# The second product of a sine block, from sixteen full pieces to seven half-size products

## The chip, the cores and the metric

The kernel runs on one core of a Trainium2 chip. The metric is the device time of one execution in microseconds (us), the median of several runs. TensorE (PE) multiplies, VectorE (DVE), ScalarE (ACT) and GpSimd (POOL) work on elements, SyncE (SP) issues nearly all DMA transfers; SBUF is the working memory on the chip, PSUM takes the sums of PE in eight banks of 128 x 512 floats.

## The reference

Block-local attention over 64-token chunks gives `x` (4608 tokens x 512). Then `u = ((x @ w1) * (x @ w2)) @ w3 @ w_o`, and the part that is changed here, the sine block:

```python
def _moe2_ref(x, w_in, w_out):
    h = x @ w_in                      # 4608 x 512 @ 512 x 2048
    g = h * np.cos(h)
    return (g @ w_out).astype(np.float32)   # 4608 x 2048 @ 2048 x 512
```

All weights come as 64-bit floats and are decoded on the chip. For precision every operand of a product is split into two float16 halves, high and low, and a product is three matmuls: high x high, low x high, high x low.

## The kernel before

The 4608 tokens are nine blocks of 512. Three kinds of work follow each other and overlap at their borders: attention with the first products (`ab`, `u_of`) for all blocks, then the sine blocks. Between them `w_in` and `w_out` are surveyed (largest value) and converted to float16 halves in DRAM (`convert_in`, `convert_out`).

A sine block has two products. The first, `h_of`, is by seven half-size products (the scheme of Winograd and Strassen): `u` is combined into seven operands by `combined`, the seven operands of `w_in` are made once and fetched again for every block (`fetch_in`, 896 KB a transfer). Per block there are four steps `f_`; a step makes seven products of 12 matmuls with 256 columns into the banks x, y, z of `ps_h`. ACT copies a partial result from PSUM to SBUF (`kept`, L1278), DVE adds another one from PSUM (`plus`, L1284), and so arise four quarters c11, c21, c22, c12 of `h`. `finish` then makes g = h cos(h) of each quarter: round with a magic number (ACT L1296), subtract (DVE L1300), absolute value (L1306, or ACT L1304), sine (ACT L1309), multiply (L1312, on DVE or POOL), and two halves in float16 (ACT L1315, DVE L1318).

The second product, `y_of`, is plain: 4 tiles of 128 tokens x 16 pieces of `w_out` x 3 matmuls with 512 columns (L1351 to L1353), 192 a block, into two banks; ACT scales the sum (L1358), SP stores it (L1361). All of `w_out` lies in SBUF (32 KB of each partition, `wout_p`), fetched once by `fetch`; `gh_p` holds g of two blocks.

Nothing is ordered by hand: every operation is recorded by `op(engine, cost, priority, ...)`, and `Plan.order` places all of them by a list schedule with the costs given in the code (`MM`, `LAT`, `ISSUE`, `DMA_RATE`), the priorities and the free places of the buffer pools. The order of each engine that comes out is fixed; on the chip an engine runs its queue in that order and waits on semaphores. y of a block is placed among the first product of the next block by its priority (`start_h`, `period`, `Y0`).

Of the kernel before, what the change touches and what calls it, by code (L numbers as in the profile page):

```python
# [11 lines left out]
F32 = mybir.dt.float32  # L12
# [11 lines left out]
MAGIC = 12582912.0  # L24

# [39 lines left out]
class Plan:  # L65
# [50 lines left out]
    def order(self):  # L116
# [26 lines left out]
        now, done, wakes, order, on_psum = 0.0, 0, [0.0], [], False  # L143
# [12 lines left out]
        while done < len(ops):  # L156
# [11 lines left out]
            for e in ENGINES:  # L168
# [35 lines left out]
                if e == "DVE":  # L204
                    if not o.psum:
                        o.cost += SHARED * max(0.0, free["POOL"] - now)
                    on_psum = o.psum
                elif e == "POOL" and free["DVE"] > now and not on_psum:
                    o.cost += SHARED * (free["DVE"] - now)
# [7 lines left out]
                for s in o.succ:  # L217
                    s.left -= 1
                    there = end if list(s.alts) == [e] and e != "SP" else end + LAT[e]
                    s.ready = max(s.ready, there)  # L220
                    if not s.left:
                        for a in s.alts:
                            heapq.heappush(pending[a], (s.ready, s.prio, s.n))
                        heapq.heappush(wakes, s.ready)
                for b in o.bufs:
                    left[id(b)] -= 1
                    ends[id(b)] = max(ends.get(id(b), 0.0), end + LAT[e])
# [28 lines left out]
def fused_kernel(  # L256
# [36 lines left out]
    R0, R1, C0, C1, A0, A1, A2, A3, I0, I1, I2, I3, I4, I5, F0, F1, Y0 = 0.9, 10.9, 16.5, 27.6, 60.0, 6, 70.0, 10.6, 240.5, 10.0, 28.1, 510.5, 5.6, 11.6, 8.4, -26.5, 55.8  # L293
# [69 lines left out]
    ps_h = bank_pool(0, 1, 2, 3, 4, 5, queue=True)  # L363
    ps_y = bank_pool(6, 7)
# [26 lines left out]
    def operand(a):  # L391
# [4 lines left out]
        operand, *line("XHL", 0, 2 * KB, 7), *line("W12", 52 * KB, 2 * KB, 2), *line("RES", 10 * KB, 2 * KB, 3), *line("WG", 32 * KB, 2 * KB, 4), queue=True  # L396
# [16 lines left out]
    wout_p = sbuf_pool(halves_of, ("CONV", 0, 32 * KB))  # L413
    uin_p = sbuf_pool(chunks, ("XHL", 14 * KB, 8 * KB), queue=True)
    gh_p = sbuf_pool(halves_of, ("W12", 0, 32 * KB), ("WG", 0, 32 * KB), queue=True)
    hs_p = sbuf_pool(plain, *line("W12", 32 * KB, 2 * KB, 10), queue=True)
    r_p = sbuf_pool(plain, *line("RES", 0, 2 * KB, 5))
    yo_p = sbuf_pool(plain, *line("TMP", 0, 2 * KB, 2))
# [29 lines left out]
    period = 8 * pair + 16 * 12 * MM  # L448
# [4 lines left out]
    with tc.manual_schedule():  # L453
        ident = const.tile([P, P], F32, name="ident")
        make_identity(nc, ident)
        half_pi = const.tile([P, 1], F32, name="half_pi")
        nc.gpsimd.memset(half_pi, math.pi / 2)
        magic = const.tile([P, 1], F32, name="magic")
        junk = const.tile([P, 512], mybir.dt.bfloat16, name="junk")
        nc.gpsimd.memset(magic, MAGIC)  # L460
# [596 lines left out]
        def u_scales(first, last, prio):  # L1057
# [5 lines left out]
            def f():  # L1063
                nc.vector.tensor_scalar(t[:, 0], inv, wsc[0][2], 2.0 / math.pi, ALU.mult, ALU.mult)
                nc.vector.tensor_scalar(t[:, 1], s, wsc[0][1], 8.0 * math.pi * c * 2.0 ** (-2 * TOP), ALU.mult, ALU.mult)
                nc.vector.tensor_scalar(t[:, 2], inv, wsc[0][2], wsc[1][2], ALU.mult, ALU.mult)
                nc.vector.tensor_scalar(t[:, 2], t[:, 2], 2.0 ** (2 * TOP - 2) / c, None, ALU.mult)
# [37 lines left out]
        wout_dram = dram.tile([16, P, 2 * 512], F16, name="wout_dram")  # L1105
# [51 lines left out]
        def two_parts(at, raw, n, scale, goes, name, place):  # L1157

            dst = Buf(two_p, name)
            def f():  # L1160
                nc.scalar.activation(dst.ap[:, 0], value(raw, n), AF.Copy, scale=scale[1])
            op("ACT", 0.72, at, f, r=[(raw, n), scale[0]], w=[dst])
            def f():
                nc.vector.scalar_tensor_tensor(dst.ap[:, 1], value(raw, n), scale[1], dst.ap[:, 0], ALU.mult, ALU.subtract)
            op("DVE", 0.75, at, f, r=[(raw, n), scale[0], dst], w=[dst])
            def f():
                nc.sync.dma_start(place, dst.ap.rearrange("p s e -> p (s e)"))
            op("SP", 0.6, at, f, r=[dst], w=[goes], size=P * 2 * KB)

        def convert_out(prio, step):  # L1170
            for n in range(16):
                at = prio + step * n
                two_parts(at, decoded(at, 1, n, raw2_p), 0, wsc[1][:2], (kept, n), f"wo_{n}", wout_dram[n])
# [52 lines left out]
        def fetch(prio):  # L1226

            b = wpart[1] = Buf(wout_p, "wout")
            for c in range(4):
                def f(c=c):  # L1230
                    nc.sync.dma_start(
                        b.ap[:, 4 * c : 4 * c + 4].rearrange("p n s e -> p n (s e)"),
                        wout_dram[4 * c : 4 * c + 4].rearrange("n p e -> p n e"),
                    )
                ns = range(4 * c, 4 * c + 4)
                op("SP", 0.6, prio + c, f, r=[(kept, n) for n in ns], w=[(b, n) for n in ns], size=P * 8 * KB, after=[px_of[NTILE - 1]])
# [13 lines left out]
        def h_of(bl):  # L1250
# [6 lines left out]
            tg = gh[bl] = Buf(gh_p, f"gh{bl}")  # L1257
            half, unit = T // 2, step / 7
            for f_ in range(K2 // 4):
# [26 lines left out]

                def finish(n, side, hs, pr=pr, f_=f_):
                    r = Buf(r_p, f"r{bl}_{f_}{n}{side}")
                    ns = slice(8 * n + 2 * f_, 8 * n + 2 * f_ + 2)
                    def part(s):  # L1290
                        return tg.ap[:, ns, s, side * half : (side + 1) * half]
                    def value():
                        return hs.ap.rearrange("p (f t) -> p f t", f=2)
                    key = (8 * n + 2 * f_, side)
                    def f():
                        nc.scalar.activation(r.ap, hs.ap, AF.Identity, bias=magic)  # L1296
                    op("ACT", 0.71, pr, f, r=[hs], w=[r])
# [3 lines left out]
                    op("DVE", 0.74, pr, f, r=[hs, r], w=[r])  # L1301
                    def f(eng):
                        if eng == "ACT":
                            nc.scalar.activation(r.ap, r.ap, AF.Abs)  # L1304
                        else:
                            nc.vector.tensor_scalar(r.ap.bitcast(U32), r.ap.bitcast(U32), 0x7FFFFFFF, None, ALU.bitwise_and)  # L1306
# [4 lines left out]
                    def f(eng):  # L1311
                        engines[eng].tensor_tensor(out=hs.ap, in0=hs.ap, in1=r.ap, op=ALU.mult)  # L1312
                    op(TT, 0, pr, f, r=[hs, r], w=[hs])
                    def f():
                        nc.scalar.activation(part(0), value(), AF.Copy, scale=sg[1])  # L1315
                    op("ACT", 0.72, pr, f, r=[hs, sg[0]], w=[(tg, (0, key))])
                    def f():
                        nc.vector.scalar_tensor_tensor(part(1), value(), sg[1], part(0), ALU.mult, ALU.subtract)  # L1318
                    op("DVE", 0.76, pr, f, r=[hs, sg[0], (tg, (0, key))], w=[(tg, (1, key))])
# [113 lines left out]
```

## Time and profile before

| | |
|---|---|
| median of 3 runs | 1449.78 us (1448.88 to 1451.02) |
| profiled execution: its time, its span | 1456.48 us, 1454.7 us |
| PE busy, share of the span | 1413.4 us, 97% |
| DVE, ACT, POOL busy | 992.3 us, 997.8 us, 347.1 us |
| chain that ended last | PE 87%, DVE 5%, ACT 4%, DMA 3%, issue 1% |
| largest lines of the chain | L1269 (first product) 21%, L975 (`ab`) 20%, L1351 to L1353 (second product) 8% each |
| DMA | 192.97 MB on SP's queue, 41.8% of 16 engines |

The sine blocks fill the second half of the span, from about 730 us on. Busy time says how long an engine had an instruction in work; what an instruction costs a queue that is full is the distance from its start to the start of the next one, which is less, because the end of one overlaps the beginning of the next. The chain names what each step of the end waited for. Matmul records can be missing by a few per cent, so counts of matmuls are taken from the code.

### The profile page before, as it was taken

The numbers are of one execution on the slowest core, as the hardware profiler recorded it, in microseconds if no ns is written. First come the engines' busy times: TensorE is split into PE (matmuls) and PEld (weight loads), VectorE is DVE, ScalarE is ACT, GpSimd is POOL, SyncE is SP. The second block draws the span as 40 slices with busy tenths as digits, with TensorE's granted clock in tenths as the row PEclk, the third lists the DMA queues.
The fourth block names the chain that finished last, engine by engine and source line by source line (L and its number), as shares of the span: only waits on it lengthen the run. The fifth ranks groups of instructions, "written<-read, shape, count | busy, mean of one in ns | idle before, by whom it ended". The sixth has DMA issues, their size and how long they took to land.

```text
span 1454.7 us, 28969 instructions
## 1 busy us (share of the span) xinstructions
PE 1413.4 (97%) x11683; PEld 979.5 (67%) x11688; DVE 992.3 (68%) x1587; ACT 997.8 (69%) x2152; POOL 347.1 (24%) x250
## 2 busy tenths in 40 slices
PE   5789999999999999999999999999999999999998
PEld 4346768777777768686876777666666666666644
DVE  8779788468997654578589888757485756454510
ACT  5688777678887676697488888667585756574610
POOL 0000014122653111124145342313141322122100
PEclk8989999999999999999999999999999999999999
DMA  9951383227679222275534443333151333333000
GB/s 313 266 116 44 105 292 84 65 68 221 192 224 264 66 60 66 66 216 180 193 106 174 156 160 144 138 116 145 67 194 67 145 109 117 116 116 116 16 22 29
DMA packets 170454, 194.81 MB, mean 134 GB/s; under 512 B 118992, under 2 KB 133328, under 8 KB 169168
## 3 DMA queue, kind: packets, MB, share of 16 engines
q1 hardware_dynamic: 170320, 192.97, 41.8%
q8 instruction: 91, 1.49, 0.4%
q14 instruction: 43, 0.35, 0.1%
HBM read 162.53 MB, written 30.41 MB: 133 GB/s over the span
## 4 chain that ended last, share of the span: by engine, by line
PE 87%; DVE 5%; ACT 4%; DMA 3%; issue 1%; POOL 0%; ACTq 0%; POOLq 0%; SPq 0%
PE ps L1269 21%; PE ps L975 20%; PE ps L1353 8%; PE ps L1351 8%; PE ps L1352 8%; PE ps L1085 4%; PE ps L1086 4%; PE ps L1087 4%; PE ps L923 2%; PE ps L716 2%; PE ps L779 1%; PE ps L731 1%; DMA u_dram<-TMP 1%; PE ps L764 1%; ACT ATT L748 1%
## 5 line engine op out<-in xcount | busy, mean ns | idle before, releaser
L975 PE MATMUL ps<-XHL,W 128*128 128x256 f16 x3024 | 348.9, 273 | 4.9 <-ACT RES L482 4.7
L1269 PEld LDWEIGHTS <-ATT 128*128 128x128 f16 x3024 | 295.7, 98 | 61.2 <-issue 2.3
L975 PEld LDWEIGHTS <-W 128*128 128x128 f16 x3024 | 293.1, 98 | 45.0 <-issue 5.9
L1312 POOL TENSOR_TENSOR W<-W,RES 128x512 f32<-128x512 f32 x105 | 149.6, 1432 | 411.5 <-ACT RES L1309 405.6
L1278 ACT ACTIVATE W<-ps,smalls 128x512 f32<-128x512 f32 x144 | 97.8, 679 | 114.4 <-PE ps L1269 113.9
L1269 PE MATMUL ps<-XHL,ATT 128*128 128x256 f16 x1392 | 167.8, 273 | 1.1 <-ACT W L1278 0.9
L1284 DVE SCALAR_TENSOR_TENSOR W<-ps,smalls,W 128x512 f32<-128x512 f32 x108 | 80.2, 746 | 101.8 <-PE ps L1269 67.4
L482 ACT ACTIVATE RES<-ps,smalls 128x512 f32<-128x512 f32 x126 | 87.1, 697 | 62.8 <-PE ps L975 58.8
L1300 DVE SCALAR_TENSOR_TENSOR RES<-RES,W 128x512 f32<-128x512 f32 x144 | 109.9, 768 | 22.4 <-ACT RES L1296 21.0
L1010 POOL TENSOR_TENSOR WG<-RES,WG 128x512 f16<-128x512 f32 x44 | 58.0, 1324 | 270.6 <-DMA ATT<-in_v_dram 157.5
L1351 PE MATMUL ps<-CONV,W 128*128 128x512 f16 x320 | 121.4, 379 | 0.0
L1353 PE MATMUL ps<-CONV,W 128*128 128x512 f16 x320 | 121.4, 379 | 0.0
L1352 PE MATMUL ps<-CONV,W 128*128 128x512 f16 x320 | 121.4, 379 | 0.0
L1296 ACT ACTIVATE RES<-W,magic 128x512 f32<-128x512 f32 x144 | 102.5, 716 | 27.1 <-DVE W L1284 25.1
L1309 ACT ACTIVATE RES<-RES,half_pi 128x512 f32<-128x512 f32 x144 | 102.6, 715 | 15.1 <-DVE RES L1306 13.8
L995 DVE SCALAR_TENSOR_TENSOR RES<-ps,smalls,RES 128x512 f32<-128x512 f32 x108 | 79.8, 744 | 45.8 <-ACT RES L482 26.8
L1085 PE MATMUL ps<-WG 128*128 128x512 f16 x288 | 109.4, 380 | 0.0
L1086 PE MATMUL ps<-WG 128*128 128x512 f16 x288 | 109.3, 379 | 0.0
L1087 PE MATMUL ps<-WG 128*128 128x512 f16 x288 | 109.3, 379 | 0.0
L748 ACT ACTIVATE ATT<-ps,SMALL 128x64 f32<-128x64 f32 x288 | 85.8, 327 | 21.4 <-DVE SMALL L743 21.4
L1351 PE MATMUL ps<-CONV,WG 128*128 128x512 f16 x256 | 97.2, 380 | 0.0
L1352 PE MATMUL ps<-CONV,WG 128*128 128x512 f16 x256 | 97.1, 379 | 0.0
(186 smaller groups left out, 2504.9 us busy)
## 6 DMA issues: line engine op xcount, KB each, us to landing
ATT<-win_dram SPq DMA_DIRECT2D x72, 896.0 KB, 5.9
CONV<-in_moe_w_in_dram SPq DMA_DIRECT2D x32, 512.0 KB, 6.8
CONV<-in_moe_w_out_dram SPq DMA_DIRECT2D x32, 512.0 KB, 6.7
ATT<-in_v_dram SPq DMA_DIRECT2D x144, 64.0 KB, 2.5
u_dram<-TMP SPq DMA_DIRECT2D x36, 256.0 KB, 2.7
XHL<-u_dram SPq DMA_DIRECT2D x9, 1024.0 KB, 5.4
out_dram<-TMP SPq DMA_DIRECT2D x36, 256.0 KB, 2.0
ATT<-in_q_dram SPq DMA_DIRECT2D x32, 256.0 KB, 3.7
```

The lines of the kernel that those rows point to most:

```text
L975: nc.tensor.matmul(ps.ap[:, p * half : (p + 1) * half], w12[j, g].ap[:, b, w_, c, p * P : (p + 1) * P], t[a].ap[:, c, u_], start=(not more ...
L1085: nc.tensor.matmul(ps.ap, wh.ap[:, kk, 0, ns], g[:, 0], start=(kk == 0), stop=False)
L1086: nc.tensor.matmul(ps.ap, wh.ap[:, kk, 0, ns], g[:, 1], start=False, stop=False)
L1087: nc.tensor.matmul(ps.ap, wh.ap[:, kk, 1, ns], g[:, 0], start=False, stop=(kk == K1 - 1))
L1269: nc.tensor.matmul(ps.ap[:, p * half : (p + 1) * half], wins[p].ap[:, b, k, w_], t[a].ap[:, k, u_], start=(not more and p == 0 and k == 0 ...
L1296: nc.scalar.activation(r.ap, hs.ap, AF.Identity, bias=magic)
L1300: nc.vector.scalar_tensor_tensor(r.ap, r.ap, -MAGIC, hs.ap, ALU.add, ALU.subtract)
L1309: nc.scalar.activation(r.ap, r.ap, AF.Sin, bias=half_pi, scale=-2.0 * math.pi)
L1312: engines[eng].tensor_tensor(out=hs.ap, in0=hs.ap, in1=r.ap, op=ALU.mult)
L1351: nc.tensor.matmul(ps.ap, tg.ap[:, kk, 0, js], wout.ap[:, kk, 0], start=(kk == 0), stop=False)
L1352: nc.tensor.matmul(ps.ap, tg.ap[:, kk, 0, js], wout.ap[:, kk, 1], start=False, stop=False)
L1353: nc.tensor.matmul(ps.ap, tg.ap[:, kk, 1, js], wout.ap[:, kk, 0], start=False, stop=(kk == K2 - 1))
```

## The change

The second product is made by seven half-size products too. It has four parts.

`finish` ends with g in float32, in the place of h, and with a sign that differs between quarters on and off the diagonal (two ACT biases, `quarters`; the rounding moves from ACT to a DVE `tensor_scalar`, and the absolute value is gone). `part` makes the two halves of an operand; `add` sums two quarters. A step makes seven operands: c11, c12, c22 as they are, and four partial sums. In blocks 0 to 7 two of the four sums of a step are adding transfers that POOL issues (`accum_op=ALU.add`), the other two are on DVE; in block 8 all four are on DVE.

`y_of` makes seven products of 48 matmuls with 256 columns into the banks x (5), y (6) and z (7), with the same `kept` (ACT) and `plus` (DVE). `ps_h` has five banks and not six.

`convert_out` makes seven operands of `w_out` (four sums of quarter pieces on DVE, then halves) and starts earlier (I3 is 430.0, it was 510.5). `fetch` brings one operand, 1 MB, for each product of each block: 63 transfers into three places.

In the planner a POOL transfer counts as a transfer; the sums of `combined` for u run on DVE alone. Orders of all five engines are new from about the fifth `ab` block on; before it they are as they were.

```diff
-    ps_h = bank_pool(0, 1, 2, 3, 4, 5, queue=True)
-    ps_y = bank_pool(6, 7)
+    ps_h = bank_pool(0, 1, 2, 3, 4, queue=True)
+    ps_y = {n: bank_pool(5 + i) for i, n in enumerate("xyz")}
...
+    wout_p = sbuf_pool(lambda a: a.bitcast(F16).rearrange("p (k s e) -> p k s e", k=8, s=2), *line("CONV", 0, 8 * KB, 3), queue=True)
+    gop_p = sbuf_pool(one_half, *line("W12", 0, 2 * KB, 24), *line("WG", 0, 2 * KB, 8), queue=True)
...
-    period = 8 * pair + 16 * 12 * MM
+    period = 16 * pair
...
+        def fetch(bl, o, prio):
+            b = Buf(wout_p, f"wout{bl}_{o}")
+            def f():
+                nc.sync.dma_start(b.ap.rearrange("p k s e -> p (k s e)"), wout_dram[o].rearrange("p k e -> p (k e)"))
...
+                def part(o, hs, pr=pr, f_=f_):
+                    d = tg[o, f_] = Buf(gop_p, f"g{bl}_{f_}_{o}")
+                    def f():
+                        nc.scalar.activation(d.ap[:, 0], hs.ap, AF.Copy, scale=sg[1])
...
+                        nc.vector.scalar_tensor_tensor(d.ap[:, 1], hs.ap, sg[1], d.ap[:, 0], ALU.mult, ALU.subtract)
...
+                def add(a, b, way, pr=pr):
+                    if way:
+                        def f():
+                            nc.gpsimd.dma_start(a.ap, b.ap, accum_op=ALU.add)
+                        op("POOL", 1.2, pr, f, r=[a, b], w=[a], size=2 * P * 2 * KB)
+                    else:
+                        def f():
+                            nc.vector.tensor_tensor(out=a.ap, in0=a.ap, in1=b.ap, op=ALU.add)
+                        op("DVE", 0.7, pr, f, r=[a, b], w=[a])
...
-                        nc.scalar.activation(r.ap, hs.ap, AF.Identity, bias=magic)
+                        nc.vector.tensor_scalar(r.ap, hs.ap, 0.25, MAGIC, ALU.add, ALU.add)
...
-                    op({"DVE": 0.5, "ACT": 0.69}, 0, pr, f, r=[r], w=[r])
...
-                        nc.scalar.activation(r.ap, r.ap, AF.Sin, bias=half_pi, scale=-2.0 * math.pi)
+                        nc.scalar.activation(r.ap, r.ap, AF.Sin, bias=quarters[side], scale=(2 * side - 1) * TURN)
...
-                        engines[eng].tensor_tensor(out=hs.ap, in0=hs.ap, in1=r.ap, op=ALU.mult)
+                        nc.vector.tensor_tensor(out=hs.ap, in0=hs.ap, in1=r.ap, op=ALU.mult)
...
+                way = [bl < NB - 1 and i in (1, 3) for i in range(4)]
+                add(c11, c21, way[0])
+                add(c21, c22, way[1])
+                part(5, c11)
+                add(c22, c11, way[2])
+                part(3, c21)
+                add(c12, c22, way[3])
+                part(4, c22)
+                part(6, c12)
...
-                            nc.tensor.matmul(ps.ap, tg.ap[:, kk, 0, js], wout.ap[:, kk, 0], start=(kk == 0), stop=False)
...
+                w = fetch(bl, b, prio + i * unit - Y1)
...
+                                    nc.tensor.matmul(
+                                        ps.ap[:, j * 256 : (j + 1) * 256], g[:, u_, n, j * P : (j + 1) * P], w.ap[:, 2 * f_ + n, w_],
...
+            multiply(x, 0, 0, 0)
+            c11 = kept(x, "m1", 0)
+            multiply(y, 1, 1, 1)
+            plus(y, c11, 1)
+            store(c11, 0, 0, 1)
+            multiply(x, 4, 4, 2, True)
+            c21 = kept(x, "u2", 2)
+            multiply(z, 5, 5, 3)
+            multiply(x, 3, 3, 4, True)
+            c22 = kept(x, "v5", 4)
+            plus(z, c22, 4)
...
+            multiply(x, 6, 2, 5, True)
...
+            multiply(z, 2, 6, 6, True)
```

The order of DVE in a late sine block before, where the quarters of one step are finished (L1284 `plus`, L1300 and L1306 of `finish`, L1312 the product with the sine, L1318 the low half):

```order
L1284 SCALAR_TENSOR_TENSOR W_67<-ps_7706,smalls,W_67 128x512
L1306 TENSOR_SCALAR RES<-RES 128x512
L1312 TENSOR_TENSOR W_67<-W_67,RES 128x512
L1300 SCALAR_TENSOR_TENSOR RES<-RES,W_67 128x512
L1306 TENSOR_SCALAR RES<-RES 128x512
L1318 SCALAR_TENSOR_TENSOR W_67<-W_67,smalls 128x2x256
```

The order of DVE in a sine block of the changed kernel, from one sum on DVE (L1330) to the next one of the same step; between the two lies an adding transfer of POOL, which reads and writes quarters that the two touch (L1345 product with the sine, L1336 and L1339 rounding, L1320 low half of an operand, L662 and L666 the next block's u, L1414 `plus` of y):

```order
L1330 TENSOR_TENSOR W_67<-W_67,RES 128x512
L1345 TENSOR_TENSOR WG<-WG,RES 128x512
L1336 TENSOR_SCALAR RES<-WG 128x512
L1339 SCALAR_TENSOR_TENSOR RES<-RES,WG 128x512
L1320 SCALAR_TENSOR_TENSOR WG<-W_67,smalls,WG 128x512
L662 SCALAR_TENSOR_TENSOR RES<-TMP,smalls,RES 128x2x256
L662 SCALAR_TENSOR_TENSOR XHL<-XHL,smalls 128x2x256
L1345 TENSOR_TENSOR WG<-WG,RES 128x512
L666 TENSOR_TENSOR XHL<-XHL 128x2x256
L1414 SCALAR_TENSOR_TENSOR CONV<-ps_78,smalls,CONV 128x512
L1330 TENSOR_TENSOR RES<-RES,W_67 128x512
```

The product with the sine is on DVE alone now, the low halves are seven for four, and an adding transfer has the time of the rows between two sums before DVE asks for it.

SP's queue in a late block before (L1222 `w_in`, L1361 store, L1245 u):

```order
L1361 DMA out_dram<-TMP 128x512
L1222 DMA ATT<-win_dram 128x3584 x2
L1245 DMA XHL<-u_dram 128x2048
L1361 DMA out_dram<-TMP 128x512
L1222 DMA ATT<-win_dram 128x3584 x2
L1361 DMA out_dram<-TMP 128x512
```

SP's queue in the changed kernel (L1261 `w_out`, 1 MB each; L1253 `w_in`, L1420 store):

```order
L1261 DMA CONV<-wout_dram 128x4096 x2
L1420 DMA out_dram<-CONV 128x2x256
L1261 DMA CONV<-wout_dram 128x4096 x3
L1253 DMA ATT<-win_dram 128x3584
L1420 DMA out_dram<-CONV 128x2x256
L1253 DMA ATT<-win_dram 128x3584
L1261 DMA CONV<-wout_dram 128x4096
L1420 DMA out_dram<-CONV 128x2x256
```

Seven transfers of 1 MB a block now stand among the eight of 896 KB, and behind stores that wait for ACT and DVE.

## Rows read from the trace of the kernel before

**Rows 1.** Windows: us, busy (instructions) of PE, PEld, DVE, ACT, POOL, PEclk, DMA share, GB/s.

```profile
811.95:890.07 78.12, 78.12 (x577) 56.27 (x576) 68.18 (x91) 69.13 (x112) 28.54 (x19) 1.00 0.45 172
1124.43:1202.55 78.12, 78.12 (x530) 51.66 (x529) 52.09 (x69) 50.65 (x79) 19.36 (x14) 1.00 0.33 122
730.00:1455.00 725.00, 719.50 (x4826) 471.89 (x4824) 455.37 (x619) 464.24 (x728) 191.89 (x131) 1.00 0.30 113
```

**Rows 2.** Waits of PE from 730 us on: us in total, times, longest.

```profile
PE ps L1269 <- ACT W L1278: 0.9, 1, 0.9
PE ps L1269 <- DVE W L1284: 0.3, 1, 0.3
```

**Rows 3.** Chain in order of time: start, us, what; a stretch of first-product matmuls.

```profile
862.65 7.86 PE ps L1269 x72
```

**Rows 4.** Timeline of PE: start, us, what; the second product's matmuls in a row.

```profile
1388.55 0.38 PE L1351 MATMUL ps<-CONV,WG 128*128 128x512 f16 x1
1388.76 0.38 PE L1352 MATMUL ps<-CONV,WG 128*128 128x512 f16 x1
1388.98 0.38 PE L1353 MATMUL ps<-CONV,WG 128*128 128x512 f16 x1
1389.19 0.38 PE L1351 MATMUL ps<-CONV,WG 128*128 128x512 f16 x1
```

**Rows 5.** Groups of instructions, 780 to 1455 us: weight loads of the first product.

```profile
L1269 PEld LDWEIGHTS <-ATT 128*128 128x128 f16 x2736 | 267.5, 98 | 56.1 <-issue 2.0
```

**Rows 6.** Timeline of DVE in a late sine block.

```profile
1144.59 0.75 DVE L1318 SCALAR_TENSOR_TENSOR WG<-W,smalls,WG 128x512 f16<-128x512 f32 x1
1145.25 0.69 DVE L1300 SCALAR_TENSOR_TENSOR RES<-RES,W 128x512 f32<-128x512 f32 x1
1145.86 0.75 DVE L659 SCALAR_TENSOR_TENSOR XHL<-XHL,smalls 128x512 f16<-128x512 f32 x1
1146.52 0.42 DVE L1306 TENSOR_SCALAR RES<-RES 128x512 uint32<-128x512 uint32 x1
...
1147.69 0.75 DVE L1284 SCALAR_TENSOR_TENSOR W<-ps,smalls,W 128x512 f32<-128x512 f32 x1
1148.36 0.42 DVE L1306 TENSOR_SCALAR RES<-RES 128x512 uint32<-128x512 uint32 x1
1149.26 0.69 DVE L1312 TENSOR_TENSOR W<-W,RES 128x512 f32<-128x512 f32 x1 [0.48 <-ACT RES L1309]
1149.87 0.69 DVE L1300 SCALAR_TENSOR_TENSOR RES<-RES,W 128x512 f32<-128x512 f32 x1
...
1153.32 1.74 DVE L1318 SCALAR_TENSOR_TENSOR WG<-W,smalls,WG 128x512 f16<-128x512 f32 x1
```

**Rows 7.** Timeline of POOL at the last of those rows.

```profile
1153.24 1.27 POOL L1312 TENSOR_TENSOR W<-W,RES 128x512 f32<-128x512 f32 x1 [1.45 <-ACT RES L1309]
```

**Rows 8.** Windows of 20 us around the conversion and in the first sine blocks.

```profile
560.00:580.00 20.00, 20.00 (x246) 17.62 (x247) 10.18 (x16) 12.51 (x36) 4.19 (x4) 1.00 0.19 44
640.00:660.00 20.00, 20.00 (x236) 17.76 (x234) 18.28 (x29) 18.88 (x60) 8.07 (x6) 1.00 0.70 203
760.00:780.00 20.00, 20.00 (x149) 14.34 (x147) 19.16 (x23) 17.06 (x30) 10.43 (x7) 1.00 0.44 159
840.00:860.00 20.00, 20.00 (x150) 14.47 (x148) 18.67 (x25) 18.24 (x29) 9.15 (x7) 1.00 0.56 215
```

**Rows 9.** DMA issues from 820 to 1400 us: count, KB each, median us to landing.

```profile
ATT<-win_dram SPq DMA_DIRECT2D x58, 896.0 KB, 6.0
out_dram<-TMP SPq DMA_DIRECT2D x30, 256.0 KB, 2.0
XHL<-u_dram SPq DMA_DIRECT2D x5, 1024.0 KB, 8.1
```

**Rows 10.** Lines of the conversion on DVE: duration ns min/median/max, first and last start.

```profile
L1150 DVE SCALAR_TENSOR_TENSOR CONV<-CONV x32: 675/694/1766, 211.6 to 693.7; 128x512 uint32<-128x512 uint32 x32
L1164 DVE SCALAR_TENSOR_TENSOR CONV<-CONV,smalls x16: 739/746/1859, 622.4 to 699.1; 128x512 f16<-128x512 f32 x16
```

More of the change, by code (lines that the diff above doesn't have):

```diff
@@ L24 @@
 MAGIC = 12582912.0
+TURN, QUARTER = 6.283185005187988, 1.5707962512969971
 MM = 0.2155
@@ L142, in order @@
         dma = 0.0
-        now, done, wakes, order, on_psum = 0.0, 0, [0.0], [], False
+        now, done, wakes, order, on_psum, port = 0.0, 0, [0.0], [], False, 0.0
         def place(b, taken):
@@ L205, in order @@
                     if not o.psum:
-                        o.cost += SHARED * max(0.0, free["POOL"] - now)
+                        o.cost += SHARED * max(0.0, port - now)
                     on_psum = o.psum
-                elif e == "POOL" and free["DVE"] > now and not on_psum:
-                    o.cost += SHARED * (free["DVE"] - now)
+                elif e == "POOL" and not o.size:
+                    if free["DVE"] > now and not on_psum:
+                        o.cost += SHARED * (free["DVE"] - now)
+                    port = now + o.cost
                 order.append(o)
@@ L218, in order @@
                     s.left -= 1
-                    there = end if list(s.alts) == [e] and e != "SP" else end + LAT[e]
+                    there = end if list(s.alts) == [e] and not o.size else end + LAT["SP" if o.size else e]
                     s.ready = max(s.ready, there)
@@ L1155, in value, with convert_out @@
             return raw.ap[:, :, n].bitcast(F32)
-        def two_parts(at, raw, n, scale, goes, name, place):
-            dst = Buf(two_p, name)
+        def convert_out(prio, step):
+            bs, s = wsc[1][:2]
+            fb, fs = small([P, 2], "so4")
             def f():
[L1161 to L1173, printed above, removed]
+                nc.vector.tensor_scalar(fs[:, :1], s, 0.25, None, ALU.mult)
+                nc.vector.tensor_scalar(fs[:, 1:], s, -0.25, None, ALU.mult)
+            op("DVE", 0.3, prio, f, r=[bs], w=[fb])
+            def side(raw, n, h):
+                return raw.ap[:, 256 * h : 256 * h + 256, n].bitcast(F32)
@@ L1321, in h_of @@
+                    op("DVE", 0.7, pr, f, r=[hs, r], w=[hs])
                 multiply(x, 0, 0, "x1")
@@ new lines, in two, with kept, f, plus @@
+            def two(a):
+                return a.rearrange("p (j e) -> p j e", j=2)
+            def kept(ps, name, i):
+                b = Buf(yo_p, f"y{name}{bl}")
+                def f():
+                    nc.scalar.activation(b.ap, two(ps.ap), AF.Copy, scale=iy[1])
+                op("ACT", 0.69, prio + i * unit, f, r=[ps, iy[0]], w=[b])
+                return b
+            def plus(ps, b, i):
+                def f():
+                    nc.vector.scalar_tensor_tensor(b.ap, two(ps.ap), iy[1], b.ap, ALU.mult, ALU.add)
+                op("DVE", 0.75, prio + i * unit, f, r=[ps, iy[0], b], w=[b])
@@ new lines, in store, with f @@
+            def store(b, side, n, i):
+                def f():
+                    rows = out[bl * T + side * 256 : bl * T + side * 256 + 256, n * 256 : n * 256 + 256]
+                    nc.sync.dma_start(rows.rearrange("(j p) e -> p j e", j=2), b.ap)
+                op("SP", 0.6, prio + i * unit, f, r=[b], size=P * 2 * KB)
+            multiply(x, 0, 0, 0)
[4 more added lines that the diff above has]
+            multiply(x, 4, 4, 2, True)
```

150 lines of the change are left out of this document (80 added, 70 removed).

## Prediction

> **What bounds the kernel now.** I read the windows first, then the waits of PE, the timelines, and the transfers last. From 730 us on PE is busy 719.5 of 725.0 us, and in a steady sine block 78.12 of 78.12 us, at a granted clock of 1.00, which is 2.4 GHz; DVE is busy 52.1 us and ACT 50.7 us of such a block [rows 1]. The waits say the same: in this half of the kernel PE waits 0.9 us for ACT once and 0.3 us for DVE once [rows 2]. So a matmul taken away here is time taken away, as long as nothing that feeds PE becomes late. The change takes matmul columns away and fills DVE and the transfers for it; the forecast is about how much of the first is lost to the second.
>
> **The matmuls.** A matmul with 256 columns costs 7.86 / 72 = 0.1091 us in a row [rows 3]; one with 512 columns costs 0.215 us by the distances in the timeline (1388.55 to 1389.19 us in three steps, 0.213; over a whole block 78.12 - 336 x 0.1091 = 41.46 us for 192 of them, 0.2159, which I use) [rows 1, 4]. The second product of a block goes from 192 x 0.2159 = 41.46 us to 7 x 48 = 336 matmuls of 0.1091 us, 36.66 us. That is 4.80 us a block and 43.2 us in nine. The new matmuls have the shape of the first product's, which loads a weight of 98 ns beside each matmul of 109 ns [rows 5] and holds its pace, so I count nothing for the 144 more loads a block. A block is then 2 x 36.66 = 73.3 us of PE.
>
> **DVE.** Distances from start to start give what an instruction costs a full queue: a low half (as L1318) 0.66, L1300 and L1312 0.61, `plus` (L1284) 0.67, the one-input L1306 at most 0.42 us [rows 6]. By the code a steady block has 12 `plus`, 16 each of the two rounding steps and the product with the sine, 28 low halves, 8 sums, 3 `plus` of y, and 11 for the next u: 8.0 + 6.7 + 9.8 + 9.8 + 18.5 + 4.9 + 2.0 + 7.0 = 66.7 us, 91% of 73.3 us. Before, it is 52.1 us, part of which is stretch: where DVE and POOL add together an instruction of DVE takes 1.74 us, not 0.75 [rows 6, 7]. POOL does no elementwise work in the new sine blocks, so this stretch goes. ACT needs 71 x 0.70 = 50 us a block and is no candidate.
>
> 91% leaves 6.6 us a block, but not from the start. Block 0 has no y beside it. From the first `plus` to the last of block 1, the order has 119 us of DVE work, and 118 us of matmuls. There PE waits for almost every moment that DVE idles, less the few microseconds that the free banks give. The fullest 20 us of the trace are 19.16 us of DVE beside a full PE [rows 8], 96%; at 95% these two blocks take it 119 / 0.95 = 125 us, 7 more than PE. I count 6 us; bounds are 0 (the free banks cover it) and 14 us (at 87%, the share from 811.95 to 890.07 us [rows 1], DVE takes 19 us more than PE, of which I leave 5 to the banks).
>
> **The adding transfers.** 64 of them, and none in the trace, nor any transfer that POOL issues. In the order of DVE I added up, for each, the work between the instruction it waits for and the first that waits for it, by the distances above: 1.3 to 10.3 us, in the middle 6.5 us. That is the cover. The nearest rows for the transfer: 2.0 us for a store of the same 256 KB alone, 8.1 us for 1 MB behind two others, 6.0 us for 896 KB in pairs [rows 9]. At 5 us from end to end the sum of what is missing is 10 us over all 64, at 6 us 28, at 7 us 62, at 8.1 us 116. I take 6 us, in the middle: a small transfer, but among large ones and with POOL's part ahead of it. The 28 us are 3.5 us a block, within DVE's 6.6 us to spare; a quarter reaches PE, 7 us. Bounds: 0 at 2.0 us, and (116 / 8 - 6.6) x 8 = 63 us at 8.1 us.
>
> By the Trainium skill ("DMA: Bandwidth & Descriptors", section on the anatomy of a DMA on the software path) a transfer issued by POOL takes about 2.0 us plus its bytes by 436 GB/s, with some 1 us to the first byte; my estimate from this page is 3.6 to 4.2 us, and the sum would lose the 7 us. The same skill speaks against the change in another place ("SBUF — State Buffer", section on who interferes with whom): a one-input DVE instruction in its two-port mode shuts POOL out, and POOL cannot write descriptors meanwhile. By it each adding transfer can start up to one rounding step (L1336) later. The trace shows a conflict of this pair of engines only the other way, DVE stretched by POOL's sums; if the rule holds, the transfer is up to 0.42 us longer, the missing sum goes from 28 to about 40 us, and PE's part from 7 to 10.
>
> **Other transfers.** A block fetches 7.3 MB of `w_in`, now 7.3 MB of `w_out`, 1 MB of u, and stores 1 MB: 16.8 MB, with 8 x 0.5 MB for the sums 21 MB in 73.3 us, 286 GB/s. At 215 GB/s the engines' share is 0.56 [rows 8], so this is 0.75 of them; the trace has PE full beside 0.70 [rows 8]. `w_out` has three places. Between the last matmul that reads an operand and the first that reads what replaces it, PE has 6.7 us of work in four of 60 cases, under 9 us in eleven and about 20 us in the median, by the order and 0.109 us each. Against a landing of 6.0 us all fit; against 8.1 us seven are short by about 1 us each, some more when a store ahead in SP's queue waits. I count 3 us, between 0 and 15.
>
> **The rest.** At the end, after the last product of h, PE has 264 matmuls, 28.8 us; the operands of the last sums are ready before their turn (eleven matmul groups stand ahead, 10.5 us, against some 9 us of DVE work). But bank x is read by ACT between two products, and twice nothing stands between: 2 x 0.9 us, the one such wait in the trace [rows 2]. Last comes a `plus` and a store in place of an ACT copy and a store, the same. `convert_out` adds 32 sums of half width (some 0.4 us, by half of 0.69 [rows 10]) and 16 low halves, 24 us of DVE, and runs one block earlier. Where it was, DVE is at 18.28 of 20 us and PE full; where it goes there is room, 10.18 of 20 us [rows 8]. I count 1 us, between 0 and 5. Up to there the order is the old one, so nothing is gained or lost before.
>
> **The sum.** 1456.5 us for the profiled execution (1454.7 of span and 1.8 around it), - 43.2 for matmuls, + 6 for the first two blocks, + 7 for adding transfers, + 3 for `w_out`, + 1.8 at the end, + 1 for the conversion: 1432.1 us. The median of the runs is 6.7 us under the profiled one, so 1425 us.
>
> **Rivals.**
> 1. *Everything is covered.* The transfers take 5 us or less, and DVE's small slack is enough; PE stays full as it is now. For it: PE was full beside 96% of DVE [rows 8]. Against: never for two whole blocks. 1449.8 - 43.2 + 1.8 + about 3 = 1411 us.
> 2. *DVE is the bound.* At 7 us a transfer DVE misses 62 us, all it has to spare, or POOL's issuing stretches DVE as its sums do now by 1 us each [rows 6, 7]. Then the sine blocks run at DVE's pace, about 2 us a block over PE's, and the start costs 14: 1449.8 - 43.2 + 1.8 + 16 + 14 = 1438 us.
> 3. *The adding transfers are late, and the kernel is slower.* At the 8.1 us that a transfer behind two others takes, DVE, in order, stands in front of each sum or half; 63 us as above, and 9 for the start and `w_out` as in the forecast: 1449.8 - 43.2 + 1.8 + 63 + 9 = 1480 us. It turns to slower where the misses exceed 6.6 + 41 / 8 = 11.7 us a block, 1.5 us each, at a transfer of about 7.7 us. For it: 0.75 of the DMA engines' time is in use. Against: 256 KB is a quarter of the transfer that took 8.1.
> 4. *The matmuls do not shrink.* If the new ones needed 0.1234 us (41.46 / 336) instead of 0.1091, nothing would be gained: 1449.8 + 1.8 + 14 = 1466 us. Against it speak the first product's, all of the same shape [rows 3, 5].
>
> **Chances.** Forecast 0.42, rival 1 0.27, rival 2 0.16, rival 3 0.13, rival 4 0.02. The time is that of the forecast, 1425 us. The range goes from 1408 us (all matmuls' gain, less the end) to 1452 us, which leaves out most of rivals 3 and 4. 0.2%, 3 us, is about what the runs can tell from no change. Rivals 3 and 4 are slower, 0.15 together; a part of 0.02 lies near zero, between rival 2 and 3; faster is 0.83.
>
> **What would show it.** Right: 256-column matmuls of the second product at 0.109 us, blocks of 73 to 76 us with a full PE in the later ones, DVE 63 to 68 us in each, waits of PE of some 10 to 20 us in all, most of them in the first two blocks, and an adding transfer of about 6 us. If PE waits under 6 us, rival 1; blocks of 75 us or more throughout with DVE over 95%, rival 2; DVE idle before L1330 and L1320 with a transfer as the releaser, over 10 us a block, rival 3. Waits of PE's `w_out` lines for transfers above 15 us would upset the sum from a side where I expect little.

## The result, and the profile after

The changed kernel takes 1465.9 us (median of four runs, 1461.5 to 1470.6), the kernel before 1450.4 us in the same session: ratio 1.0106, interval 1.007 to 1.0142. It is 1.1% slower where 1.7% faster was forecast, outside the range. Rival 3, with a chance of 0.13, comes nearest to what happened.

The profiled execution is 1461.5 us, its span 1459.5 us. The page's busy times and its DMA queues (share of 16 engines last):

```profile
PE 1378.7 (94%) x12984; PEld 1104.1 (76%) x12984; DVE 1172.3 (80%) x2015; ACT 958.2 (66%) x2090; POOL 224.2 (15%) x193
...
q1 hardware_dynamic: 187264, 257.99, 54.9%
q0 software_dynamic: 9216, 16.78, 6.5%
```

Windows, with the columns of [rows 1]: the sine stage before, and then in the changed kernel the whole sine stage, the stretch that stood in [rows 1], and three short ones.

```profile
732.00:1454.70 722.70, 717.50 (x4817) 470.95 (x4815) 453.37 (x617) 463.73 (x727) 190.44 (x131) 1.00 0.31 113
```

```profile
732.00:1459.50 727.50, 684.97 (x6095) 597.37 (x6092) 611.22 (x1001) 414.75 (x646) 55.72 (x64) 0.99 0.70 223
811.95:890.07 78.12, 71.84 (x652) 63.40 (x650) 71.31 (x117) 46.63 (x74) 6.00 (x7) 1.00 0.73 234
900.00:920.00 20.00, 17.70 (x146) 14.82 (x145) 15.30 (x25) 10.26 (x16) 1.72 (x2) 0.91 0.97 313
1125.00:1130.00 5.00, 1.91 (x9) 1.28 (x10) 3.10 (x5) 3.74 (x6) 0.00 (x0) 0.79 0.00 0
1130.00:1135.00 5.00, 5.00 (x42) 4.20 (x40) 4.33 (x8) 1.64 (x3) 0.86 (x1) 0.86 0.56 147
```

From 732 us on PE idles 727.5 - 685.0 = 42.5 us; before, the same sum gives 722.7 - 717.5 = 5.2 us. DVE isn't full either (611 of 727.5 us). The matmuls did shrink: a row of 120 of them, in the chain that ended last, gives 13.11 / 120 = 0.109 us each.

```profile
1424.82 13.11 PE ps L1393 x120
```

The waits of PE from 730 us on (total, times, longest), where [rows 2] had 1.2 us in all:

```profile
PE ps L1393 <- DVE W L1320: 9.5, 9, 1.7
PE ps L1393 <- ACT W L1317: 8.9, 4, 4.3
PE ps L1296 <- ACT WG L1305: 6.4, 4, 3.0
PE ps L1393 <- ACT CONV L1408: 4.5, 3, 2.9
PE ps L1393 <- DMA CONV<-wout_dram: 2.5, 2, 1.3
...
```

PE waits for the halves of an operand (L1317 ACT, L1320 DVE). What these two wait for is in their own waits; a DMA whose output and input are quarters is an adding transfer:

```profile
ACT W L1317 <- DMA WG<-WG: 24.8, 11, 5.6
ACT W L1317 <- DMA W<-W: 18.9, 6, 5.0
ACT WG L1317 <- DMA WG<-WG: 8.4, 5, 3.2
...
```

```profile
DVE WG L1330 <- DMA WG<-WG: 18.8, 8, 3.9
DVE W L1330 <- DMA W<-W: 9.9, 3, 3.7
...
```

With the smaller groups ACT waits 77.7 us and DVE 40.4 us, 118 us together. Some of these waits run side by side: on the clock, at least one of the two engines waits for an adding transfer during 86 us. DVE waits as a writer: the third sum (L1330) overwrites c22, which the transfer of the second sum still reads. The transfers themselves (time of POOL's issue in ns min/median/max; the last line, for all 64, counts from the start of the issue to the landing):

```profile
L1326 POOL DMA_DIRECT2D WG<-WG x30: 850/859/1207, 754.2 to 1354.5; - x30
...
DMA to landing us min/median/max: 3.2/5.2/10.6
```

The median hides two groups: of the 64 transfers 31 land in under 5 us and 27 in 7.3 to 10.6 us. What tells them apart, for the most part, is the traffic that a transfer meets. I counted from the trace how busy the packets of SP's queue keep the 16 DMA engines in the first 3.2 us after an issue: under a quarter of the time for 22 transfers, which land in 3.2 to 4.5 us (median 3.3), and over three quarters for 29, which land in 4.6 to 10.6 us (median 8.7). Two that follow each other, issued at 1110.55 us (share 0.00) and at 1116.76 us (share 0.80); KB and us to landing last:

```profile
WG<-WG POOLq DMA_DIRECT2D x1, 256.0 KB, 3.2
WG<-WG POOLq DMA_DIRECT2D x1, 256.0 KB, 9.4
```

The 27 late transfers stand behind 106 of the 118 us. The second of the two in the timeline (start, us; idle before and its releaser in brackets):

```profile
1116.76 0.86 POOL L1326 DMA_DIRECT2D WG<-WG  x1 [5.35 <-ACT W L1305]
1119.86 0.72 ACT L1342 ACTIVATE RES<-RES,quarter 128x512 f32<-128x512 f32 x1 [0.42 <-DVE RES L1339]
1126.15 1.95 ACT L1317 ACTIVATE W<-WG,smalls 128x512 f16<-128x512 f32 x3 [5.57 <-DMA WG<-WG]
1126.90 2.08 DVE L1320 SCALAR_TENSOR_TENSOR W<-WG,smalls,W 128x512 f16<-128x512 f32 x3 [4.15 <-ACT W L1317]
1127.54 0.28 PE L1393 MATMUL ps<-CONV,W 128*128 128x256 f16 x1 [4.29 <-ACT W L1317]
```

POOL issues at 1116.76 us; ACT is through with what stands ahead 4 us later and stops, DVE stops behind ACT, PE behind both; some 9 us after the issue all go on. The granted clock is 0.79 in the window of 5 us in which PE's wait ends and 0.86 in the next one, means between its levels of 1.2 and 2.4 GHz. Other transfers slowed as well: a store of 256 KB, 2.0 us in [rows 9], now has a median of 6.9 us.

```profile
CONV<-wout_dram SPq DMA_DIRECT2D x63, 1024.0 KB, 7.2
...
out_dram<-CONV SPq DMA_DIRECT2D x36, 256.0 KB, 6.9
```

The profiled executions differ by 1461.54 - 1456.48 = +5.1 us. For the account I count each sine stage from its own first matmul, at 732.36 us before, at 729.67 us in the changed kernel and at 732.08 us in e5 below, a run of the same matmuls without long waits. The changed kernel and e5:

```profile
729.67:1459.50 729.83, 687.30 (x6111) 599.02 (x6109) 613.42 (x1004) 416.65 (x649) 55.72 (x64) 0.99 0.69 222
732.08:1413.30 681.22, 674.56 (x6111) 597.13 (x6109) 614.44 (x965) 488.48 (x752) 0.00 (x0) 1.00 0.58 213
```

PE's idle time in the stage is +37.3 us. The same matmuls keep PE busy 687.3 us and not 674.6: +12.7 for the slow clock. The matmuls are -43.2, and the stage begins 2.7 us earlier. That is +4.1 of the +5.1 us.

### The profile page after: what moved, and what is told of

The parts are those of the page before. It is cut to its first block, busy times and chain, and to the rows that moved or that the text cites. A ratio compares the mean times of both kernels' runs of the same rounds, so it can differ in the third digit from the quotient of the medians.

```text
span 1459.5 us, 32138 instructions
## 1 busy us (share of the span) xinstructions
PE 1378.7 (94%) x12984; PEld 1104.1 (76%) x12984; DVE 1172.3 (80%) x2015; ACT 958.2 (66%) x2090; POOL 224.2 (15%) x193
## 3 DMA queue, kind: packets, MB, share of 16 engines
q1 hardware_dynamic: 187264, 257.99, 54.9%
q0 software_dynamic: 9216, 16.78, 6.5%
## 5 line engine op out<-in xcount | busy, mean ns | idle before, releaser
L978 PEld LDWEIGHTS <-W 128*128 128x128 f16 x3024 | 292.6, 98 | 45.5 <-issue 7.4
L1393 PE MATMUL ps<-CONV,W 128*128 128x256 f16 x2304 | 278.0, 275 | 24.7 <-DVE W L1320 9.5
L1393 PEld LDWEIGHTS <-W 128*128 128x128 f16 x2304 | 225.6, 98 | 57.5 <-DVE W L1320 11.9
L1342 ACT ACTIVATE RES<-RES,quarter 128x512 f32<-128x512 f32 x144 | 102.9, 717 | 98.0 <-DVE RES L1339 97.8
L1296 PE MATMUL ps<-WG,ATT 128*128 128x256 f16 x768 | 96.0, 274 | 4.8 <-ACT WG L1305 3.3
L1317 ACT ACTIVATE W<-WG,smalls 128x512 f16<-128x512 f32 x99 | 68.4, 713 | 37.2 <-DMA WG<-WG 24.8
L1393 PE MATMUL ps<-CONV,WG 128*128 128x256 f16 x720 | 88.1, 274 | 1.5 <-ACT CONV L1408 0.8
L1296 PE MATMUL ps<-RES,ATT 128*128 128x256 f16 x624 | 79.1, 273 | 0.9 <-ACT WG L1305 0.9
L1393 PEld LDWEIGHTS <-WG 128*128 128x128 f16 x720 | 70.4, 98 | 10.8 <-issue 1.2
L1320 DVE SCALAR_TENSOR_TENSOR W<-WG,smalls,W 128x512 f16<-128x512 f32 x99 | 71.7, 746 | 6.0 <-ACT W L1317 5.8
L662 DVE SCALAR_TENSOR_TENSOR XHL<-XHL,smalls 128x512 f16<-128x512 f32 x84 | 68.6, 837 | 8.2 <-ACT XHL L659 7.9
```

Source lines behind the costliest of these rows:

```text
L662: nc.vector.scalar_tensor_tensor(d.ap[:, :, 1], ap(x), scale[1], d.ap[:, :, 0], ALU.mult, ALU.subtract)
L978: nc.tensor.matmul(ps.ap[:, p * half : (p + 1) * half], w12[j, g].ap[:, b, w_, c, p * P : (p + 1) * P], t[a].ap[:, c, u_], start=(not more ...
L1296: nc.tensor.matmul(ps.ap[:, p * half : (p + 1) * half], wins[p].ap[:, b, k, w_], t[a].ap[:, k, u_], start=(not more and p == 0 and k == 0 ...
L1320: nc.vector.scalar_tensor_tensor(d.ap[:, 1], hs.ap, sg[1], d.ap[:, 0], ALU.mult, ALU.subtract)
L1342: nc.scalar.activation(r.ap, r.ap, AF.Sin, bias=quarters[side], scale=(2 * side - 1) * TURN)
L1393: nc.tensor.matmul(ps.ap[:, j * 256 : (j + 1) * 256], g[:, u_, n, j * P : (j + 1) * P], w.ap[:, 2 * f_ + n, w_], start=(not more and f_ == ...
```

## The experiments

T1: the adding transfers land late because they share the DMA engines with `w_in` and the new stream of `w_out`; ACT and DVE, in order, stop at their readers, PE behind them. T2: DVE's fullness is the cause. T3: a transfer issued by POOL takes its 5 us whatever surrounds it. A cut of an operation or another time in the planner gives new orders; of all runs only e1 keeps those of the changed kernel. Summary (waits: ACT + DVE for adding transfers, added; idle: PE from 732 us to the end of the span):

| run | median us | ratio to before, interval | waits us | landing us, min/median/max | PE idle us |
|---|---|---|---|---|---|
| changed kernel | 1465.9 | 1.0106 (1.0070 to 1.0142) | 118 | 3.2/5.2/10.6 | 42.5 |
| e1, 64 bytes | 1424.4 | 0.9818 (0.9788 to 0.9847) | 36 | 2.0/4.7/8.8 | 15.1 |
| e4, `w_out` kept | 1422.1 | 0.9815 (0.9774 to 0.9857) | 37 | 3.2/3.6/10.0 | 12.8 |
| e6, both | 1414.2 | 0.9749 (0.9725 to 0.9773) | 11 | 2.0/2.1/7.8 | 8.6 |
| e3, all sums on DVE | 1435.8 | 0.9903 (0.9874 to 0.9933) | - | - | 22.9 |
| e7, last sum only | 1433.1 | 0.9859 (0.9834 to 0.9885) | 21 | 3.2/3.9/7.7 | 20.0 |
| e10, second sum only | 1434.0 | 0.9880 (0.9860 to 0.9899) | 63 | 3.3/3.7/9.1 | 19.9 |
| e2, 6.2 us planned | 1569.1 | 1.0814 (1.0791 to 1.0837) | 35 | 3.2/3.8/12.5 | 108.4 |
| e8, e2 and `w_out` kept | 1536.6 | 1.0584 (1.0564 to 1.0603) | 7 | 3.2/3.4/8.3 | 91.7 |
| e9, e7 and 6.2 us planned | 1424.8 | 0.9815 (0.9800 to 0.9829) | 0 | 3.3/3.9/7.3 | 16.2 |
| e5, e3 and rounding shared | 1414.7 | 0.9738 (0.9718 to 0.9758) | - | - | 6.7 |
| e11, e5 and e9 | 1411.3 | 0.9721 (0.9706 to 0.9736) | 0 | 3.2/3.5/9.4 | 6.3 |

**e1: small transfers.**

```diff
-                            nc.gpsimd.dma_start(a.ap, b.ap, accum_op=ALU.add)
+                            nc.gpsimd.dma_start(a.ap[:, :16], b.ap[:, :16], accum_op=ALU.add)
```

> The order of all engines is that of the changed kernel; each adding transfer moves 64 bytes per partition and not 2 KB, so most of two of the four partial sums of g stays out of the output. Theory T1 (the adding transfers land late because their 256 KB share the DMA engines with w_in and the w_out stream, ACT and DVE wait in order for them, PE waits for ACT and DVE, and the granted clock falls behind the long waits): the idle time of PE goes from 42 us to under 20 and the time to 1420 to 1435. Rival T2 (VectorE, at 611 us of 727, is itself what PE waits for): nothing to gain from the transfer, 1460 to 1468. Rival T3 (a POOL-issued transfer takes about 5 us whatever it carries): ACT and DVE wait as before, 1455 to 1466.

T1's time, and T2 falls: ACT, DVE and POOL run the changed kernel's order place by place, DVE is busy 609 us (it was 611), and 41.5 us are gone. The landing tells more: with a thirty-second of the bytes the shortest falls to 2.0 us and the median by 0.5 only. What falls is the number of the late ones: 12 land after more than 7 us where it was 27, and where SP's queue fills over three quarters of the first 3.2 us the median is 6.6 us and not 8.7. The cover is 6.5 us in the middle, which fits with most of the waits being gone.

```profile
DMA to landing us min/median/max: 2.0/4.7/8.8
```

**e4: no `w_out` stream.**

```diff
-                w = fetch(bl, b, prio + i * unit - Y1)
+                w = held_w.get(i % 3) or held_w.setdefault(i % 3, fetch(bl, b, prio + i * unit - Y1))
```

> The w_out operands are fetched three times in all and these three are used for every product, so some 7 MB of transfers less per block (the output is another one; the amount of arithmetic and the order of the products stay). T1: with DMA share down from 0.70 to about 0.4 in the sine stage the adding transfers land in 3 to 4 us and not 5.2 (median), waits of ACT and DVE for them fall from 115 us to under 50, time 1420 to 1435. T2: 1460 to 1468. T3: the landings stay at about 5 us and so does the time, 1455 to 1466.

The transfers carry all their bytes and land in 3.6 us at the median, 8 of 64 after more than 7 us; DVE has the same work, and 44 us are gone. T3 falls here, and T2 again. But the order is not the old one, though I had expected it: without the fetches the list schedule comes out otherwise. From about 796 us on PE mixes the two products in another way, and 400 of ACT's 2090 places and 727 of DVE's 2015 hold another instruction. How much of the 44 us is the traffic and how much the order, this run doesn't show.

```profile
DMA to landing us min/median/max: 3.2/3.6/10.0
```

**e6: both cuts.**

> Both cuts at once: adding transfers of 64 bytes per partition, and w_out operands fetched three times in all (most of two partial sums and the true w_out operands are left out). With 64 bytes alone an adding transfer still took 4.7 us at the median (shortest 2.0), with w_out kept alone 3.6 (shortest 3.2). If these 4.7 us are mostly queueing among the bulk traffic (T1), the median with both cuts is 2.0 to 2.8 us and the waits for them fall to nearly nothing, time 1410 to 1422. If they are the fixed cost of a transfer issued by POOL (T3), the median stays at 4 to 4.7 us.

```profile
DMA to landing us min/median/max: 2.0/2.1/7.8
```

The orders of ACT, DVE and POOL are those of e4. So some 2.0 us are there for any such transfer, about 1.2 to 1.5 for its 256 KB (3.2 - 2.0 by the shortest, 3.6 - 2.1 by the medians), and the rest, up to 10.6 us in the changed kernel, is the other traffic. By the Trainium skill ("DMA: Bandwidth & Descriptors", the anatomy of a DMA on the software path) a transfer that POOL issues has a fixed part of some 2.0 us; the shortest of 2.0 and the median of 2.1 us agree with it.

**e3: all sums on DVE.**

```diff
-                way = [bl < NB - 1 and i in (1, 3) for i in range(4)]
+                way = [False] * 4
```

> No adding transfers: all four partial sums of every block of g are added by VectorE, about 4 instructions of 0.67 us more for each of 16 blocks' sums that the transfers made, so VectorE stands near 71.6 us of 73.3 in a block. T1: the waits for transfers are gone and in-order waits between PE, ACT and DVE stay short, 1425 to 1445, faster than the changed kernel although VectorE is fuller. T2: slower than the changed kernel, 1470 or more. T3: as T1.

A fuller DVE is faster than the adding transfers. But now it is the bound: in the window of a steady block DVE is busy 98.33 of 100 us, and PE idles at the start too.

```profile
732.00:800.00 68.00, 60.68 (x486) 48.04 (x484) 62.96 (x108) 46.48 (x74) 0.00 (x0) 0.96 0.42 155
900.00:1000.00 100.00, 97.85 (x890) 86.77 (x888) 98.33 (x161) 64.08 (x96) 0.00 (x0) 1.00 0.58 213
```

**e7 and e10: one transfer a step,** the last sum (e7, the first line) or the second (e10, the second line).

```diff
+                way = [bl < NB - 1 and i == 3 for i in range(4)]
+                way = [bl < NB - 1 and i == 1 for i in range(4)]
```

> Only one of the four partial sums goes by an adding transfer, the last (32 transfers and not 64); the other three on VectorE, which stands near 69 of 73.3 us. T1: half the transfers, so about half of the 115 us of waits, or less since the last sum has most work behind it; 1430 to 1448. T2: fuller VectorE, slower than the changed kernel, over 1466.

> One adding transfer per group, but the second sum and not the last (the planner as in the changed kernel). Its result is read by ScalarE's high half, and its source is overwritten by VectorE's third sum, so both engines wait for this transfer; for the last sum only ScalarE waits. In the changed kernel VectorE waited 40 us, all of it L1330, the sum that overwrites a source. T1 with this: VectorE waits about 30 to 40 us for transfers here and not 0 as with the last sum alone, ScalarE some 20 to 40, time 1436 to 1455, slower than with the last sum alone. If only the number of transfers counts: the same as with the last sum alone, 1428 to 1438.

DVE waits 0 us for transfers in e7 and 21 us in e10 (30 to 40 expected), all at L1330: that the source is overwritten costs DVE a wait is shown. My expectation of the time was wrong: e10 waits three times as long and the two times can't be told apart. PE idles 20.0 and 19.9 us, so the further waits of e10 did not reach it.

```profile
DVE WG L1330 <- DMA WG<-WG: 9.3, 5, 2.7
DVE W L1330 <- DMA W<-W: 7.6, 3, 4.1
```

**e2 and e8: the planner told the truth.**

```diff
-LAT = {"PE": 0.35, "DVE": 0.4, "ACT": 0.4, "POOL": 0.5, "SP": 2.2}
+LAT = {"PE": 0.35, "DVE": 0.4, "ACT": 0.4, "POOL": 0.5, "SP": 2.2, "ADD": 6.2}
...
-                    there = end if list(s.alts) == [e] and not o.size else end + LAT["SP" if o.size else e]
+                    there = end if list(s.alts) == [e] and not o.size else end + LAT[("ADD" if e == "POOL" else "SP") if o.size else e]
```

> Only the planner's assumed time from an adding transfer's issue to its landing changes, from 2.2 to 6.2 us, so ACT's and DVE's readers of the sum are placed some 4 us further back in their queues, and other work goes ahead of them. T1: of the 115 us that ACT and DVE wait for the transfers about half goes, PE idles 15 to 25 us and not 42, time 1425 to 1445. T2 (VectorE's amount of work decides): the amount is the same, 1460 to 1468. T3 (fixed time of the transfer): as T1, since the order only has to allow for it; this run doesn't tell T1 from T3.

A miss by over 100 us, although the waits for adding transfers fell from 118 to 35 us. PE now waits for `w_in`:

```profile
PE ps L1296 <- DMA ATT<-win_dram: 61.4, 20, 4.1
```

SP's queue was my suspect, so e8 has e2's planner and e4's `w_out`.

> The planner with 6.2 us for an adding transfer, as in the run that took 1569 us, and in addition w_out operands fetched three times in all (the true w_out operands are left out). In that slow run the waits for adding transfers had gone from 115 to some 36 us, but PE waited 61 us for w_in, whose fetches stood in SP's queue behind w_out fetches that wait for PE. If that queue is the cause, then without the w_out fetches PE's waits for w_in vanish and the time is 1415 to 1435. If the order of the products itself is what is slow, it stays over 1500.

1537 us: the `w_out` fetches aren't the main cause; some 32 us went with them, in part perhaps by the new order that leaving them out gives. SP still stands, now at the stores that wait for DVE, and PE waits for `w_in`, ACT and DVE.

```profile
SPq L1422 <- DVE CONV L1416: 313.0, 25, 22.0
```

The slow clock has a large part in e2: counted from the stage's first matmul PE is busy 730.4 us, with a mean clock of 0.93, against 674.6 us in e5 for the same matmuls, 56 us.

**e9: the allowance with one transfer a step** (e7's line and e2's `LAT`).

> One adding transfer per group of h (the last sum), and the planner assumes 6.2 us for it. The idea: in the run with two transfers per group and 6.2 us the two follow each other (the third sum writes what the first transfer reads, the second transfer reads the result), so the allowance came twice in one chain and held h's buffers; with one transfer it comes once, at the end of the chain. T1 with this: waits for transfers fall from 21 us (one transfer, 2.2 us assumed) to under 8, the time from 1433 to 1415 to 1425. If any allowance of 6.2 us spoils the order: over 1450.

No wait for a transfer is left, and 8 us are gained over e7. So in these runs 6.2 us is a good number where it comes once in a step (e9 against e7), and a harmful one where two transfers follow each other (e2 against the changed kernel). That this is because the chain holds h's buffers is argued, not shown.

**e5 and e11: DVE relieved.** 0.25 is added when h leaves PSUM; then the first rounding step is one addition that ACT can do, and the sine needs no bias.

```diff
-                        nc.scalar.activation(b.ap, ps.ap, AF.Copy, scale=ih[1])
+                        nc.scalar.activation(b.ap, ps.ap, AF.Identity, bias=quarter, scale=ih[1])
...
-                        nc.vector.tensor_scalar(r.ap, hs.ap, 0.25, MAGIC, ALU.add, ALU.add)
+                        if eng == "ACT":
+                            nc.scalar.activation(r.ap, hs.ap, AF.Identity, bias=magic)
+                        else:
+                            nc.vector.tensor_scalar(r.ap, hs.ap, MAGIC, None, ALU.add)
...
-                        nc.scalar.activation(r.ap, r.ap, AF.Sin, bias=quarters[side], scale=(2 * side - 1) * TURN)
+                        nc.scalar.activation(r.ap, r.ap, AF.Sin, scale=(2 * side - 1) * TURN)
...
-                        nc.vector.tensor_tensor(out=hs.ap, in0=hs.ap, in1=r.ap, op=ALU.mult)
+                        nc.vector.scalar_tensor_tensor(hs.ap, hs.ap, -0.25, r.ap, ALU.add, ALU.mult)
```

> No adding transfers, as in the run with all sums on VectorE, and besides the first step of the rounding of h may go to ScalarE: 0.25 is added to h as it leaves PSUM, so that the step needs one addition only, the sine's argument needs no bias, and the product with the sine subtracts the 0.25 again. The planner gives about 100 of the 144 steps to ScalarE: VectorE loses 100 x 0.42 = 42 us in nine blocks, 4.7 a block, and stands at 67 of 73.3 us as the changed kernel does; ScalarE goes from 50 to 58 us. T1 (the waits for adding transfers are what the changed kernel lost): PE idles under 15 us, time 1415 to 1428, faster than both. T2 (a VectorE at 91% already makes PE wait some 40 us): VectorE is as full as in the changed kernel, so 1455 to 1466.

> The version with the rounding shared between VectorE and ScalarE (1414.7 us), and in it the last sum of each group by an adding transfer with 6.2 us assumed. VectorE falls by 32 x 0.67 = 21 us more. T1: PE is nearly full already, so there is little to gain, and 32 transfers may cost a few us where they land late: 1408 to 1420, within 0.5% of the version without transfers. T2 (a fuller VectorE is what still costs time): clearly faster than it, 1402 to 1409.

Both beat both kernels, by 2.6% and 2.8% against before; their intervals overlap, so the last sum's transfer in e11 is neither gain nor loss that these runs tell. In e5 DVE has more busy time in the sine stage than in the changed kernel (614 against 611 us) and PE still idles 6.7 us only, which is the second argument against T2. PE's row of 100 us in e5, and all that PE waits for in e11 from 700 us on:

```profile
900.00:1000.00 100.00, 100.00 (x918) 89.52 (x916) 97.43 (x154) 74.71 (x114) 0.00 (x0) 1.00 0.66 244
```

```profile
PE ps L1397 <- ACT CONV L1412: 1.6, 2, 0.8
PE ps L1297 <- ACT WG L1306: 0.9, 1, 0.9
```

## Why the prediction was wrong

The step that failed is the term of the adding transfers, "I take 6 us, in the middle ... a quarter reaches PE, 7 us". What it measured: the same order with small transfers (e1) is 41.5 us faster than the changed kernel; with the `w_out` fetches gone as well (e6, in another order) it is 51.7 us, and this holds the 7 us and the 3 us of `w_out`. The forecast without these two terms is 1425 - 10 = 1415 us; e6 takes 1414.2, so the sum of the other terms was near.

- *The duration* was one number, 6 us. The median of 5.2 us, in which the 0.86 us of POOL's issue are counted, is below it. But few transfers lie in the middle: 31 of 64 land in under 5 us and cost 7.5 us of waits, 27 take 7.3 to 10.6 us and cost 106. The table of covers bends upwards (28 us missing at 6, 116 at 8.1), so the late ones weigh more than the early ones give back.
- *The cover* was added up in DVE's order alone. The first reader of a sum is ACT's L1317, and ACT, at 57% in this stage (415 of 727.5 us), can reach it sooner: in the example 4 us after the issue. Two thirds of the wait is ACT's (77.7 of 118 us). How much this adds to the late landings the runs don't separate; the early half of the transfers was covered nearly whole.
- *The share that reaches PE*: PE's idle time grew by 37 us, a third of the 118 us, or 43% of the 86 us on the clock, and not a quarter. A long wait also lowers the clock, 12.7 us, for which the sum had no term.
- *The rival* had the mechanism: transfers as late as the 8.1 us behind two others. I gave it 0.13 because I asked that all be so late (7.7 us to turn slower); 27 of 64 were enough. Its turning point of 11.7 us a block is not confirmed: that sum was of DVE's order, and DVE waits 40.4 / 8 = 5.1 us a block for transfers itself, less than the 10 us named as the sign; ACT waits another 9.7. Its 1480 us is 14 us too high.
- *The traffic* was put at 0.75 of the engines' time and dismissed since PE had been full beside 0.70 [rows 8]. The measured share is 0.70, but as a mean of windows like 0.00 and 0.97 above, and the transfers meet the full ones. The fetches for PE, asked for long before, come in time beside it (2.5 us of waits); transfers with a few microseconds of cover don't.

The other terms. Matmuls 0.109 us: right (e5, 918 recorded in 100 us). The end, 1.8 us: two waits of 0.8 us, right. Refills of `w_out`, 3 us: 2.5 us of waits, right. The first two blocks, 6 us: from 732 to 860 us PE idles 5.9 us in the changed kernel, but in e6, with the same work for DVE, 0.4 us, so DVE's work alone did not cost the 6 us. Conversion, +1 us: the sine stage starts 2.7 us earlier, but it starts at 728.1 us in e1 and at 733.9 in e6, whose order up to there is the same, so a term of 1 us can't be told. Rival 2's 1438 us comes close to e3 (1435.8), where DVE has all sums and is the bound. The rule from the Trainium skill that DVE's two-port mode keeps POOL from writing descriptors ("SBUF — State Buffer", who interferes with whom) agrees with the trace, but it is small and seldom. Of POOL's 64 issues 20 have a rounding step L1336 beside them; three of these take 914, 1157 and 1207 ns, at most 0.35 us more than the median of 859, and end just after the L1336. None of the other 44 takes over 869 ns. The longest (start, us):

```profile
754.19 1.21 POOL L1326 DMA_DIRECT2D WG<-WG  x1 [24.80 <-DVE RES L1345]
754.88 0.43 DVE L1336 TENSOR_SCALAR RES<-W 128x512 f32<-128x512 f32 x1
```

## What to carry to other kernels

Price a transfer that stands in a dependency chain by the late part of its landings under the traffic that the same change adds, not by one middle number, and compare with the traffic at the moment of its issue, not with the mean; and measure its cover in the queue of the engine that asks first, which is the emptiest. If a full engine must be relieved, an engine with room may be the better place than the DMA queues. Here it was: with 103 of 144 rounding steps moved to ACT (e5) DVE had time for the sums that the 64 transfers were to take from it. Telling a list scheduler the true latency can be worse than leaving it wrong, where the latency stands twice in one chain.

## What the runs showed of the hardware

- An adding transfer of 64 bytes per partition has nearly the median of one of 2 KB among bulk traffic, 4.7 against 5.2 us, but fewer late landings (over 7 us: 12 against 27 of 64); without the `w_out` stream the medians are 2.1 and 3.6 us.
- The landing of a 256 KB adding transfer follows the traffic at its issue: median 3.3 us where SP's queue fills under a quarter of the DMA engines' time in the first 3.2 us (22 of 64), 8.7 us where it fills over three quarters (29 of 64).
- Adding transfers fill the DMA engines more per byte than fetches: 6.5% for 16.78 MB on q0, 54.9% for 257.99 MB on q1, 0.39 against 0.21% per MB.
- Idle stretches of PE of a few microseconds cost more than their own time: around a wait of 4.3 us the granted clock falls to 0.79 and 0.86 in two windows of 5 us, and the same matmuls of the sine stage keep PE busy the longer, the more it idles: 674.6 us beside 6.7 us idle (e5), 687.3 beside 42.5 (changed kernel), 730.4 beside 108.4 (e2, mean clock 0.93).
- One-input rounding steps on DVE can hold up POOL's issue of a transfer: 3 of 20 issues beside such a step take up to 0.35 us longer, none of 44 without one.
